# A fused attention, soft-MoE and squared-ReLU kernel on one Trainium2 core: three squares in four of one FFN part go to ScalarE, the last part's weight steps end two steps sooner, one product's parts are made a group sooner

## The chip, the core and the metric

The kernel runs on one core of one Trainium2 chip. The metric is device microseconds of an execution, the median of several runs; lower is better. The times and the profile of the kernel before are from the chip.

## The reference, cut to what matters

```python
x = attention(q, k, v)                 # 4 batches, 8 heads, 768 rows, head size 64
x = soft_moe(x, phi, w1, w2)           # 3072 tokens, width 512, 8 experts of 4 slots
h = x @ w_in                           # 3072x512 @ 512x2048
r = np.maximum(h, 0.0)
g = r * r
out = g @ w_out                        # 3072x2048 @ 2048x512
```

Everything is fp32. The change lies wholly in the last three lines, the FFN (feed-forward network).

## The kernel before, in words

**The FFN.** The 2048 hidden columns are worked in five parts, `WIDTHS = [256, 384, 384, 512, 512]`, numbered q = 0 to 4. The tokens lie in `ND = 6` blocks of 512. Because the MoE output is a product of small factors, `h` for 128 hidden columns and one block is one matmul (`gemm1`, line 1055, into a PSUM tile `h`). The second product is three matmuls of 512 columns per 128 hidden columns: both g and the weights are split into a high and a low fp32r part, and hi·hi, lo·hi (lines 1075, 1076) and hi·lo (line 1084) are summed into a PSUM tile `acc`. For parts 1 to 3, VectorE then adds `acc` into the running output `oacc` (line 1089).

**The gate.** `gate` (lines 1041 to 1049) turns a tile `h` into the two parts of g. ScalarE makes r = relu(h) (line 1043). The full g is made in one of two ways: by ScalarE, as the square of r, in the second half of the same `rg` tile (line 1045), or by VectorE, as max(h, 0)·r, which reads `h` in PSUM again (line 1047). ScalarE then writes the rounded high part (line 1048), and the low part is g minus the high part (line 1049), on GpSimd, or on VectorE for the last block of part 3. The argument `own` of the call on line 1056 chooses the way.

**The loop.** Lines 1325 to 1346 walk parts 0 to 3, six blocks each, four steps (m = 0 to 3) per block; k = 4d + m counts a part's steps from 0 to 23. A step issues one `gemm1` and its gate for the *next* block, then the second product of one 128-row slice of the output. The low products of slice 0 are held until slice 1. Between these, `background` is advanced by a few yields: it loads the next part's weights, converts their 64-bit words to fp32 on ScalarE and VectorE (lines 932 to 937), makes the small factor of `gemm1` (`make_u`), and then splits weights. For part 4 this is `conv_last` (lines 984 to 1009): it makes seven weight operands, with sums and differences (lines 995 and 1004, VectorE), high parts (line 1002, ScalarE) and low parts (line 1008, in turn on VectorE and GpSimd). `total` yields are spread over `room` steps (line 1329).

**The last part.** Part 4 is done by a seven-product scheme (P1, P5, P6, P3, P7, P2, P4) on pairs of token blocks: `pair` (line 1184), three times, each with 14 groups of six matmuls (lines 1207 to 1211), two groups a product; VectorE adds every group into `oacc` (line 1191). The right-hand operands are made from squares `y11, y12, y22, y21` and differences `t1` to `t4` (line 1161, VectorE) of them. `y_steps` (line 1121) is a hand-written table: every action has a slot number, slot 0 is just after group 0 of the pair. `products` makes the two `hy` matmuls of a square (line 1136), `relu` reads them on ScalarE (line 1141), `square` writes the fp32 square (line 1144), `high` its rounded part (line 1148 or 1150, ScalarE), `low` the rest (line 1156, on GpSimd in two halves or on VectorE at once). The first pair's slots from -13 on fall into the last steps of part 3.

Every engine works through its own queue in program order; semaphores hold an instruction until its inputs are there and its output tile is free. `h` and `hy` tiles share the PSUM tags `h`, `k` and `u`: a new one waits until all readers of the old one in its place are done. The `rg` tiles and the `r` tiles of `products` share two SBUF places of the tag `e`.

Of the kernel before, what the change touches and what calls it, by code (L numbers as in the profile page):

```python
# [7 lines left out]
F32 = mybir.dt.float32  # L8
# [12 lines left out]
P = 128  # L21
# [9 lines left out]
TB = 256  # L31
WIDTHS = [256, 384, 384, 512, 512]
QL = len(WIDTHS) - 1
# [7 lines left out]
def attention_moe_ffn(ctx: ExitStack, tc, qk, vx, nn, phi, w1, w2, w_in, w_out, consts, relw, out):  # L41
    nc = tc.nc
    V, G = nc.vector, nc.gpsimd
# [153 lines left out]
    def slot(tag, shape, dt, name):  # L197
        return (pre if tag[0] == "p" else stream).tile(shape, dt, tag=tag, name=name)
# [468 lines left out]
    ph = pl.rearrange("p (t g h s) -> p t h g s", g=2, h=NPR, s=NS)  # L667
# [188 lines left out]
    ex = ctx.enter_context(tc.tile_pool(name="ex", bufs=1, side="right"))  # L856
# [176 lines left out]
    ND = NBLK // 2  # L1033

    def g_of(q, d):
        i = (q * ND + d) % 2
        if i not in gbuf:
            gbuf[i] = slot(("s2", "p2")[i], [P, 2, 4, 2 * TB], F32R, f"g{i}")
        return gbuf[i]

    def gate(q, g2, js, cs, ph, rg, own=False, low=None):
        r, g = rg[:, 0], rg[:, 1]
        nc.scalar.activation(r, ph, AF.Relu)  # L1043
        if own:
            nc.scalar.activation(g, r, AF.Square)
        else:
            V.scalar_tensor_tensor(g, ph, 0.0, r, op0=ALU.max, op1=ALU.mult)  # L1047
        nc.scalar.activation(g2[:, 0, js, cs], r, AF.Square)  # L1048
        (low or (G if q else V)).tensor_tensor(g2[:, 1, js, cs], g, g2[:, 0, js, cs].bitcast(F32), op=ALU.subtract)  # L1049

    def gemm1(q, d, j):
        if j >= WIDTHS[q] // P:
            return
        ph = fps.tile([P, 2 * TB], F32, tag="k" if (q, d) == (QL - 1, ND - 1) else next(hk), name=f"h{q}_{d}_{j}", bufs=2)
        nc.tensor.matmul(ph, lhsT=wq[q]["U"][:, j * P : j * P + P], rhs=cst[:, d * 2 * TB : d * 2 * TB + 2 * TB], start=True, stop=True)  # L1055
        gate(q, g_of(q, d), j, slice(0, 2 * TB), ph, ex.tile([P, 2, 2 * TB], F32, tag="e", name=f"rg{q}_{d}_{j}", bufs=2), q in (1, 2) and j > 0, V if (q, d) == (QL - 1, ND - 1) else None)

    def gemm1_first(n):
        ph = fps.tile([P, 2, TB], F32, tag=next(hk), name=f"h0_0_0_{n}", bufs=2)
# [31 lines left out]
    def gemm2(q, d, m):  # L1091
        if m == 0 and q:
            held[0] = gemm2_hi(q, d, 0)
            return
        pa = gemm2_hi(q, d, m)
        if m == 1 and q:
            gemm2_lo(held[0], q, d, 0)
        gemm2_lo(pa, q, d, m)
# [9 lines left out]
    def region(name, k):  # L1108
        if "t" not in yt:
            yt["t"] = slot("p4", [P, 4, 2, 2 * TB], F32, "yt")  # L1110
        yt[name] = slotZ[:, 0 : 4 * TB].rearrange("p (a c) -> p a c", a=2) if k == 4 else yt["t"][:, k]
        return yt[name]

    def y_parts(name):
        n = PLACE[name]
        if n - n % 2 not in yt:
            yt[n - n % 2] = slot(("p0", "p1", "s2", "p2")[n // 2], [P, 2, 2, 2, 2 * TB], F32R, f"yop{n}")
        t = yt[n - n % 2]
        return t[:, n % 2, 0], t[:, n % 2, 1]

    def y_steps(p):

        a, b = 2 * p, 2 * p + 1
        r, at = {}, {}

        def step(slot_, f, *args):
            at.setdefault(slot_, []).append(lambda: f(*args))

        def products(y, half, chunk):
            r[y] = ex.tile([P, 2, 2 * TB], F32, tag="e", name=f"r{y}_{chunk}", bufs=2)  # L1130
            r[y, "h"] = []
            for jj in range(2):
                j = 2 * half + jj
                tag = next(hhu)
                ph = fps.tile([P, 2 * TB], F32, tag=tag, name=f"h{y}_{chunk}_{jj}", bufs=1 if tag == "u" else 2)
                nc.tensor.matmul(ph, lhsT=wq[QL]["U"][:, j * P : j * P + P], rhs=cst[:, chunk * 2 * TB : chunk * 2 * TB + 2 * TB], start=True, stop=True)
                r[y, "h"].append(ph)

        def relu(y):
            for jj in range(2):  # L1140
                nc.scalar.activation(r[y][:, jj], r[y, "h"][jj], AF.Relu)

        def square(y, k):
            nc.scalar.activation(region(y, k), r[y], AF.Square)

        def high(name, y):
            if y in r:
                nc.scalar.activation(y_parts(name)[0], r[y], AF.Square)  # L1148
            else:
                nc.scalar.copy(y_parts(name)[0], yt[y])  # L1150

        def low(name, y, eng):
            hi, lo = y_parts(name)
            for c in ((0, 1), (1, 2)) if eng is G else ((0, 2),):
                c = slice(*c)
                eng.tensor_tensor(lo[:, c], yt[y][:, c], hi[:, c].bitcast(F32), op=ALU.subtract)  # L1156
            yop[name] = hi, lo

        def diff(y, k, x0, x1):
            x0, x1 = yt[x0], yt[x1]  # L1160
            V.tensor_tensor(region(y, k), x0, x1, op=ALU.subtract)

        for y, half, chunk, slot_ in (("y11", 0, a, -13), ("y12", 0, b, -10), ("y22", 1, b, -7), ("y21", 1, a, -3)):
            step(slot_, products, y, half, chunk)
            step(slot_ + 1, relu, y)
        for y, k, slot_ in (("y11", 0, -10), ("y12", 1, -8), ("y22", 3, -5), ("y21", 1, 0)):
            step(slot_, square, y, k)
        for y, k, x0, x1, slot_ in (("t1", 2, "y12", "y11", -6), ("t2", 0, "y22", "t1", -3), ("t3", 4, "y22", "y12", -2), ("t4", 2, "y21", "t2", 3)):
            step(slot_, diff, y, k, x0, x1)
        for name, y, s0, s1, eng in (("P1", "y11", -9, -7, G), ("P5", "t1", -3, -1, G), ("P6", "t2", 0, 2, V), ("P3", "y22", -2, 1, G),  # L1170
                                     ("P7", "t3", 2, 5, G), ("P2", "y21", 1, 3, G), ("P4", "t4", 6, 8, V)):
            step(s0, high, name, y)
            step(s1, low, name, y, eng)
        return at

    plans = [y_steps(p) for p in range(ND // 2)]

    def make(p, slot_):
        for n in (p, p + 1):
            if n < ND // 2:  # L1180
                for f in plans[n].get(slot_ - (14 if n > p else 0), ()):
                    f()
# [127 lines left out]
    def background(q):  # L1310
        if q > 1:
            load_part(q)
        yield from conv_in(q)
        for _ in range(3):
            yield
        yield from make_u(q)
        if q == QL:
            yield from conv_last()
            return
        for c in conv_out(q):  # L1320
            yield from c
# [3 lines left out]
    for i in range(QL * ND):  # L1325
        q, d = i // ND, i % ND
        if d == 0:
            bg = background(q + 1)
            total, room = 5 * (WIDTHS[q + 1] // P) + (10 if q + 1 == QL else 7), 4 * (ND - 1) - (2 if q + 1 == QL else 1)
        for m in range(4):  # L1330
            k = 4 * d + m
            for _ in range((k + 1) * total // room - k * total // room):
                next(bg, None)
            if k == 4 * (ND - 1) - 2:
                for _ in bg:
                    pass
            if ahead[i]:
                gemm1(*ahead[i], m)
            if q == QL - 1:
                for slot_ in (2 * k - 48, 2 * k - 47):  # L1340
                    if slot_ >= -13:
                        make(0, slot_)
            if i:
                gemm2(q, d, m)
            else:
                next(first_products, None)
# [165 lines left out]
```

## Time and profile before

| | |
|---|---|
| median of 3 runs | 512.85 us (512.21 to 512.89) |
| profiled execution, its own time | 513.21 us |
| span in the trace of that execution | 511.4 us |
| PE (TensorE matmul) busy | 500.3 us, 98% |
| DVE (VectorE) busy | 391.9 us, 77% |
| ACT (ScalarE) busy | 335.3 us, 66% |
| POOL (GpSimd) busy | 158.1 us, 31% |
| TensorE clock granted, mean of the span | 0.999 |

Parts 0 to 3 of the FFN end near 444 us of the span, and the three pairs of part 4 fill the rest. A busy engine is not an engine at its best rate: matmul records overlap, so the rate of TensorE is read from the distance between the starts of matmuls that follow each other, and a stall from a distance that is longer.

### The profile page before, as it was taken

The page shows a single profiled execution, that of the slowest core. Times are in us where ns is not written, and L with a number is a line of the kernel's source. Part 1 is how long each engine was busy: PE and PEld are TensorE (multiplying, and loading weights), DVE is VectorE, ACT ScalarE, POOL GpSimd, SP SyncE. Part 2 cuts the span into 40 slices and gives each one's busy share as a digit, 9 for nine tenths or more (in the row PEclk, how much of TensorE's full clock was granted, in tenths as well). Part 3 has the DMA queues.
Part 4 walks back from the last instruction along what each step waited for, and adds up shares of the span by engine and source line. Part 5 has one row for each costly group of instructions (what it writes and reads, how often), then busy time and mean ns, then how long its engine had stood idle before and what let it go on. Part 6 is the DMA issues. An engine that isn't in the chain of part 4 may idle for free.

```text
span 511.4 us, 9819 instructions
## 1 busy us (share of the span) xinstructions
PE 500.3 (98%) x3517; PEld 382.0 (75%) x3517; DVE 391.9 (77%) x925; ACT 335.3 (66%) x840; POOL 158.1 (31%) x126
## 2 busy tenths in 40 slices
PE   9999999999999999999999999999999998999997
PEld 6777777687777744487887888788887876878785
DVE  7788888787887745688864765788696998579894
ACT  6987877878878402387985856576654566656650
POOL 7000000000000110000454554446644452866691
PEclk9999999999999999999999999999999999999999
DMA  8888999999994799913304040402200000013124
GB/s 278 261 283 295 365 309 326 313 330 314 318 336 139 274 357 420 406 64 126 123 1 164 1 164 2 164 2 67 97 1 1 2 0 1 1 41 124 62 104 164
DMA packets 25975, 86.93 MB, mean 170 GB/s; under 512 B 2882, under 2 KB 5442, under 8 KB 23746
## 3 DMA queue, kind: packets, MB, share of 16 engines
q1 hardware_dynamic: 25776, 86.13, 47.0%
q8 instruction: 29, 0.48, 0.4%
q14 instruction: 24, 0.20, 0.1%
q10 hardware_dynamic: 146, 0.13, 0.1%
HBM read 79.95 MB, written 6.29 MB: 169 GB/s over the span
## 4 chain that ended last, share of the span: by engine, by line
PE 53%; DVE 8%; ACT 1%; issue 0%; DVEq 0%; ACTq 0%
PE acc L1075 10%; PE acc L1076 10%; PE acc L1084 10%; PE pSO L923 3%; PE h L1055 3%; DVE rg L1047 1%; PE b2P L1211 1%; PE b2P L1208 1%; PE b2P L1209 1%; PE b1P L1211 1%; PE b0P L1211 1%; DVE oacc_p L1089 1%; PE b1P L1208 1%; PE b0P L1208 1%; PE b1P L1209 1%; PE b0P L1209 1%
## 5 line engine op out<-in xcount | busy, mean ns | idle before, releaser
L1075 PE MATMUL acc<-g,w 128*128 128x512 f32 x280 | 109.1, 390 | 0.0
L1076 PE MATMUL acc<-g,w 128*128 128x512 f32 x280 | 109.0, 389 | 0.0
L1049 POOL TENSOR_TENSOR g<-rg,g 128x512 fp32r<-128x512 f32 x56 | 75.4, 1352 | 81.8 <-DVE rg L1047 26.5
L263 ACT ACTIVATE sm<-sm,nm 128x256 f32<-128x256 f32 (+1 forms) x192 | 92.7, 487 | 1.3 <-DVE nm L248 1.3
L1084 PE MATMUL acc<-g,w 128*128 128x512 f32 x280 | 75.5, 389 | 0.0
L1043 ACT ACTIVATE rg<-h 128x512 f32<-128x512 f32 (+1 forms) x73 | 43.1, 591 | 44.0 <-PE h L1055 33.9
L248 DVE CUSTOM_DVE_ANT_0 sm<-s,mask 128x256 f32<-128x256 f32 (+1 forms) x192 | 66.8, 397 | 1.9 <-ACT sm L263 1.2
L1076 PEld LDWEIGHTS acc<-g,w 128*128 128x128 f32 x280 | 52.6, 188 | 11.0
L1084 PEld LDWEIGHTS acc<-g,w 128*128 128x128 f32 x280 | 52.6, 188 | 11.0
L1075 PEld LDWEIGHTS acc<-g,w 128*128 128x128 f32 x280 | 52.6, 188 | 10.7
L235 PE MATMUL s<-raw 64*128 64x256 f32 (+1 forms) x384 | 52.9, 397 | 0.0
L1089 DVE TENSOR_TENSOR oacc_p<-acc,oacc_p 128x512 f32<-128x512 f32 x48 | 32.4, 686 | 22.7 <-PE acc L1084 22.7
L673 POOL TENSOR_TENSOR lh<-lh 128x256 f32<-128x256 f32 x1 | 0.7, 731 | 158.4 <-PE pt L274 158.4
L1156 POOL TENSOR_TENSOR yop<-yt,yop 128x512 fp32r<-128x512 f32 x24 | 40.2, 1701 | 25.2 <-ACT yop L1148 9.0
L274 PE MATMUL pt<-con,sm 128*128 128x128 f32 x352 | 45.5, 277 | 1.6 <-ACT pT L280 1.6
L1048 ACT ACTIVATE g<-rg 128x512 fp32r<-128x512 f32 (+1 forms) x73 | 45.4, 621 | 1.6
L291 PE MATMUL o<-pT,v 128*64 128x128 f32 x704 | 44.2, 276 | 0.0
L274 PEld LDWEIGHTS pt<-con,sm 128*128 128x128 f32 x352 | 38.6, 141 | 7.3 <-ACT pT L280 2.8
L291 PEld LDWEIGHTS o<-pT,v 128*64 128x64 f32 x704 | 37.9, 137 | 6.9 <-ACT sm L263 2.1
L235 PEld LDWEIGHTS s<-raw 64*128 64x128 f32 x384 | 32.1, 194 | 14.6 <-DMA v<-in_vx 6.8
L1047 DVE SCALAR_TENSOR_TENSOR rg<-h,rg 128x512 f32<-128x512 f32 (+1 forms) x49 | 32.9, 674 | 9.6 <-ACT rg L1043 9.5
L263 ACT ACTIVATION_READ_ACCUMULATOR sm<-sm,nm 128x1 f32 x192 | 37.0, 193 | 0.0
(289 smaller groups left out, 880.0 us busy)
## 6 DMA issues: line engine op xcount, KB each, us to landing
w<-in_w SPq DMA_DIRECT2D x40, 512.0 KB, 6.6
raw<-in_qk SPq DMA_DIRECT2D x32, 384.0 KB, 5.3
w<-in_w SPq DMA_DIRECT2D x5, 2048.0 KB, 10.0
v<-in_vx SPq DMA_DIRECT2D x32, 256.0 KB, 4.3
raw<-in_qk SPq DMA_DIRECT2D x16, 320.0 KB, 5.1
win<-in_w_in SPq DMA_DIRECT2D x2, 2048.0 KB, 7.9
wout<-in_w_out SPq DMA_DIRECT2D x2, 2048.0 KB, 8.0
out_x<-oacc_p SPq DMA_DIRECT2D x15, 256.0 KB, 2.0
```

The lines of the kernel that those rows point to most:

```text
L235: nc.tensor.matmul(sc[hh][:, tt, 0:n, :], lhsT=r[r0 : r0 + D, tt, :], rhs=rhs, start=True, stop=True)
L248: V.tensor_tensor_reduce(out=sm[:, j, 0:n, :], in0=sc[hh][:, tt, 0:n, :], in1=m[:, 2:3, :] if n == 1 else m[:, 0:2, :], scale=-QK_SCALE, s ...
L263: nc.scalar.activation(sm[:, j, 0:n, :], sm[:, j, 0:n, :], AF.Exp, bias=nm[:, j : j + 1], scale=-1.0, accum_out=chunk_sums(i // NPR)[:, tt ...
L274: nc.tensor.transpose(pp[tt][:, hh, c, :], sm[:, 2 * tt + hh, c, :], ident)
L291: nc.tensor.matmul(o[hh * D : hh * D + D, tt, :], lhsT=v[:, c * 3 if tt == 0 else 1 + c, hh * D : hh * D + D], rhs=pT[:, 2 * tt + hh, c, : ...
L1043: nc.scalar.activation(r, ph, AF.Relu)
L1048: nc.scalar.activation(g2[:, 0, js, cs], r, AF.Square)
L1049: (low or (G if q else V)).tensor_tensor(g2[:, 1, js, cs], g, g2[:, 0, js, cs].bitcast(F32), op=ALU.subtract)
L1075: nc.tensor.matmul(pa, lhsT=whi[:, j, ms], rhs=ghi[:, j, :], start=j == 0, stop=False)
L1076: nc.tensor.matmul(pa, lhsT=wlo[:, j, ms], rhs=ghi[:, j, :], start=False, stop=False)
L1084: nc.tensor.matmul(pa, lhsT=whi[:, j, ms], rhs=glo[:, j, :], start=False, stop=j == J - 1)
L1156: eng.tensor_tensor(lo[:, c], yt[y][:, c], hi[:, c].bitcast(F32), op=ALU.subtract)
```

## The change

Three edits, all to tables or conditions that set who does what and when:

1. The gates of part 3 (`QL` is 4) with j > 0 take the way of line 1045 in place of line 1047, as parts 1 and 2 already do: three gates of four, 18 in all.
2. While part 3 is worked, `room` is 16 in place of 18: the 30 yields that prepare part 4 end two steps sooner.
3. P6's high part moves from slot 0 to slot -1, its low part from slot 2 to slot 1.

```diff
@@ gemm1
-        gate(..., q in (1, 2) and j > 0, V if (q, d) == (QL - 1, ND - 1) else None)
+        gate(..., 0 < q < QL and j > 0, V if (q, d) == (QL - 1, ND - 1) else None)
@@ y_steps
-        for name, y, s0, s1, eng in (("P1", "y11", -9, -7, G), ("P5", "t1", -3, -1, G), ("P6", "t2", 0, 2, V), ("P3", "y22", -2, 1, G),
+        for name, y, s0, s1, eng in (("P1", "y11", -9, -7, G), ("P5", "t1", -3, -1, G), ("P6", "t2", -1, 1, V), ("P3", "y22", -2, 1, G),
@@ loop
-            total, room = 5 * (WIDTHS[q + 1] // P) + (10 if q + 1 == QL else 7), 4 * (ND - 1) - (2 if q + 1 == QL else 1)
+            total, room = 5 * (WIDTHS[q + 1] // P) + (10 if q + 1 == QL else 7), 4 * (ND - 1) - (4 if q + 1 == QL else 1)
```

The queue of VectorE where part 3 meets part 4. The names leave out the part: `rg_4_3` is the tile of part 3, block 4, chunk 3, and `acc_3_2` the sum of part 3, block 3, slice 2; `xs` and `xp` hold the weight operands of part 4. Before:

```order
L1047 SCALAR_TENSOR_TENSOR rg_4_2_11849<-h_4_2_11847,rg_4_2_11849 128x512
L1089 TENSOR_TENSOR oacc_p_10153<-acc_3_2_11854,oacc_p_10153 128x512
L1008 TENSOR_TENSOR xs_11810<-winf_11480,xs_11810 128x512
L1047 SCALAR_TENSOR_TENSOR rg_4_3_11872<-h_4_3_11870,rg_4_3_11872 128x512
L1089 TENSOR_TENSOR oacc_p_10153<-acc_3_3_11877,oacc_p_10153 128x512
L1008 TENSOR_TENSOR xp_11811<-winf_11480,xp_11811 128x512
L1047 SCALAR_TENSOR_TENSOR rg_5_0_11897<-h_5_0_11895,rg_5_0_11897 128x512
L1049 TENSOR_TENSOR g_10196<-rg_5_0_11897,g_10196 128x512
L1008 TENSOR_TENSOR xp_11811<-winf_11480,xp_11811 128x512
L1047 SCALAR_TENSOR_TENSOR rg_5_1_11916<-h_5_1_11914,rg_5_1_11916 128x512
L1049 TENSOR_TENSOR g_10196<-rg_5_1_11916,g_10196 128x512
```

The same place after the change:

```order
L1008 TENSOR_TENSOR xs_11773<-winf_11480,xs_11773 128x512
L1089 TENSOR_TENSOR oacc_p_10153<-acc_3_0_11809,oacc_p_10153 128x512
L1089 TENSOR_TENSOR oacc_p_10153<-acc_3_1_11830,oacc_p_10153 128x512
L1008 TENSOR_TENSOR xp_11774<-winf_11480,xp_11774 128x512
L1089 TENSOR_TENSOR oacc_p_10153<-acc_3_2_11860,oacc_p_10153 128x512
L1008 TENSOR_TENSOR xp_11774<-winf_11480,xp_11774 128x512
L1089 TENSOR_TENSOR oacc_p_10153<-acc_3_3_11884,oacc_p_10153 128x512
L1047 SCALAR_TENSOR_TENSOR rg_5_0_11900<-h_5_0_11898,rg_5_0_11900 128x512
L1049 TENSOR_TENSOR g_10196<-rg_5_0_11900,g_10196 128x512
L1049 TENSOR_TENSOR g_10196<-rg_5_1_11916,g_10196 128x512
```

The products `rg_4_2`, `rg_4_3` and `rg_5_1` have left the queue, and the two low parts `xp` stand ahead of the gates of block 5, where they stood between them.

GpSimd's queue in the same place, before (`g` is the low part of a gate, line 1049):

```order
L1049 TENSOR_TENSOR g_10163<-rg_4_0_11796,g_10163 128x512
L1049 TENSOR_TENSOR g_10163<-rg_4_1_11817,g_10163 128x512
L1008 TENSOR_TENSOR xs_11810<-winf_11480,xs_11810 128x512
L1049 TENSOR_TENSOR g_10163<-rg_4_2_11849,g_10163 128x512
L1049 TENSOR_TENSOR g_10163<-rg_4_3_11872,g_10163 128x512
L1008 TENSOR_TENSOR xs_11810<-winf_11480,xs_11810 128x512
L1008 TENSOR_TENSOR xp_11811<-winf_11480,xp_11811 128x512
```

and after:

```order
L1049 TENSOR_TENSOR g_10163<-rg_4_0_11804,g_10163 128x512
L1008 TENSOR_TENSOR xs_11773<-winf_11480,xs_11773 128x512
L1049 TENSOR_TENSOR g_10163<-rg_4_1_11825,g_10163 128x512
L1008 TENSOR_TENSOR xs_11773<-winf_11480,xs_11773 128x512
L1049 TENSOR_TENSOR g_10163<-rg_4_2_11855,g_10163 128x512
L1008 TENSOR_TENSOR xp_11774<-winf_11480,xp_11774 128x512
L1049 TENSOR_TENSOR g_10163<-rg_4_3_11879,g_10163 128x512
```

All three weight parts now stand ahead of the low part of gate 4_3; one did before.

VectorE's queue in the second pair, where L1156 is P6's low part, and L1191 adds the groups 1, 2 and 3 (`12261`, `12277` or `12278`, `12289`); the other two pairs read alike:

```order
 L1191 TENSOR_TENSOR oacc_p_10153<-b1P_12261,oacc_p_10153 128x512
-L1191 TENSOR_TENSOR oacc_p_10153<-b1P_12277,oacc_p_10153 128x512
 L1156 TENSOR_TENSOR yop_12064<-yt,yop_12064 128x1024
+L1191 TENSOR_TENSOR oacc_p_10153<-b1P_12278,oacc_p_10153 128x512
 L1191 TENSOR_TENSOR oacc_p_10153<-b1P_12289,oacc_p_10153 128x512
 L1161 TENSOR_TENSOR yt<-yt 128x1024
```

P6's low part stood behind the add of group 2 and now stands ahead of it.

## Rows read from the trace of the kernel before

**Rows 1.** Busy time by stretch: PE, PEld, DVE, ACT, POOL; PE clock, DMA share, GB/s.

```profile
388.00:410.00 22.00, 22.00 (x101) 17.26 (x101) 18.01 (x26) 11.89 (x21) 7.79 (x6) 1.00 0.01 1
410.00:433.00 23.00, 20.75 (x90) 16.29 (x88) 22.34 (x28) 13.73 (x24) 10.58 (x7) 1.00 0.00 0
```

**Rows 2.** Timeline of PE, first two waits: start, us, instruction, [idle before <-releaser].

```profile
419.44 0.39 PE L1136 MATMUL hy<-cu 128*128 128x512 f32 x1
420.75 0.50 PE L1136 MATMUL hy<-cu 128*128 128x512 f32 x1 [0.91 <-DVE rg L1047]
421.08 0.39 PE L1075 MATMUL acc<-g,w 128*128 128x512 f32 x1
...
427.69 0.39 PE L1055 MATMUL h<-cu 128*128 128x512 f32 x1
...
431.28 0.39 PE L1136 MATMUL hy<-cu 128*128 128x512 f32 x1
433.05 0.50 PE L1136 MATMUL hy<-cu 128*128 128x512 f32 x1 [1.39 <-ACT ry L1141]
```

**Rows 3.** Timeline of PE, third and fourth wait.

```profile
450.41 0.39 PE L1211 MATMUL b0P<-yop,xs 128*128 128x512 f32 x1
...
451.32 0.39 PE L1209 MATMUL b0P<-yop,xs 128*128 128x512 f32 x1
452.47 0.73 PE L1211 MATMUL b0P<-yop,xs 128*128 128x512 f32 x2 [0.77 <-DVE yop L1156]
...
473.23 0.39 PE L1209 MATMUL b1P<-yop,xs 128*128 128x512 f32 x1
474.26 0.72 PE L1211 MATMUL b1P<-yop,xs 128*128 128x512 f32 x2 [0.64 <-DVE yop L1156]
```

**Rows 4.** Timeline of ACT, 415 to 433 us.

```profile
415.73 0.59 ACT L1043 ACTIVATE rg<-h 128x512 f32<-128x512 f32 x1
...
425.17 0.60 ACT L1043 ACTIVATE rg<-h 128x512 f32<-128x512 f32 x1 [1.71 <-PE h L1055]
...
430.19 0.60 ACT L1043 ACTIVATE rg<-h 128x512 f32<-128x512 f32 x1 [1.57 <-DVE g L1049]
430.82 0.63 ACT L1048 ACTIVATE g<-rg 128x512 fp32r<-128x512 f32 x1
431.36 1.04 ACT L1144 ACTIVATE yt<-ry 128x1024 f32<-128x1024 f32 x1
432.40 1.08 ACT L1141 ACTIVATE ry<-hy 128x512 f32<-128x512 f32 x2
```

**Rows 5.** Timeline of DVE: behind the first two waits, and at P6's low part.

```profile
420.01 0.68 DVE L1047 SCALAR_TENSOR_TENSOR rg<-h,rg 128x512 f32<-128x512 f32 x1
...
429.41 0.69 DVE L1049 TENSOR_TENSOR g<-rg,g 128x512 fp32r<-128x512 f32 x1
...
447.67 0.69 DVE L1191 TENSOR_TENSOR oacc<-b0P,oacc 128x512 f32<-128x512 f32 x1 [0.67 <-PE b0P L1211]
...
450.09 2.33 DVE L1156 TENSOR_TENSOR yop<-yt,yop 128x1024 fp32r<-128x1024 f32 x1
...
469.17 1.27 DVE L1191 TENSOR_TENSOR oacc_p<-b1P,oacc_p 128x512 f32<-128x512 f32 x2
```

**Rows 6.** One line's instructions: xcount: ns min/median/max, first and last start.

```profile
L1045 ACT ACTIVATE rg<-rg x24: 632/633/637, 255.9 to 357.9; 128x512 f32<-128x512 f32 x24
L1156 DVE TENSOR_TENSOR yop<-yt,yop x6: 1216/1270/2330, 450.1 to 501.7; 128x1024 fp32r<-128x1024 f32 x6
```

**Rows 7.** Timeline of POOL.

```profile
410.41 1.58 POOL L1049 TENSOR_TENSOR g<-rg,g 128x512 fp32r<-128x512 f32 x1 [1.32 <-ACT g L1048]
...
414.57 1.75 POOL L1008 TENSOR_TENSOR xs<-winf,xs 128x512 fp32r<-128x512 f32 x1
...
447.54 2.54 POOL L1156 TENSOR_TENSOR yop<-yt,yop 128x512 fp32r<-128x512 f32 x2 [2.02 <-issue]
```

**Rows 8.** Timeline of SP, the last load of weights.

```profile
354.28 0.33 SPq L948 DMA_DIRECT2D wout<-in_w_out  x1
```

More of the change, by code (lines that the diff above doesn't have):

```diff
@@ L1055, in gemm1 @@
         nc.tensor.matmul(ph, lhsT=wq[q]["U"][:, j * P : j * P + P], rhs=cst[:, d * 2 * TB : d * 2 * TB + 2 * TB], start=True, stop=True)
-        gate(q, g_of(q, d), j, slice(0, 2 * TB), ph, ex.tile([P, 2, 2 * TB], F32, tag="e", name=f"rg{q}_{d}_{j}", bufs=2), q in (1, 2) and j > 0, V if (q, d) == (QL - 1, ND - 1) else None)
+        gate(q, g_of(q, d), j, slice(0, 2 * TB), ph, ex.tile([P, 2, 2 * TB], F32, tag="e", name=f"rg{q}_{d}_{j}", bufs=2), 0 < q < QL and j > 0, V if (q, d) == (QL - 1, ND - 1) else None)
     def gemm1_first(n):
```

## The prediction

> **What bounds the kernel now.** I read three views in this order. First the stretches: around the place where part 3 of the FFN meets part 4, TensorE is busy throughout from 388 to 410 us, but only 20.75 of 23 us from 410 to 433 us, and there VectorE is busy 22.34 of the 23 us, while ScalarE has 13.73 us of work [rows 1]. The clock granted is 1.00 in both, the 2.4 GHz level, so TensorE loses there by waiting, not by its clock. Second, TensorE's timeline, for the waits themselves. From part 3 on there are four that matter. Their size is the distance between the starts of two matmuls that follow each other, less what it is without a wait: from 450.41 to 451.32 us four steps take 0.91 us, 0.227 us each [rows 3].
>
> - Wait A: 420.75 - 419.44 - 0.23 = 1.08 us; the matmul after it comes 0.33 us later, 0.10 us over the normal step, so 1.18 us together. A tile `hy` waits for VectorE's L1047 [rows 2].
> - Wait B: 433.05 - 431.28 - 0.23 = 1.54 us, 1.64 us with the same 0.10 us. A tile `hy` waits for a relu of ScalarE, L1141 [rows 2].
> - Waits C and D: 452.47 - 451.32 - 0.23 = 0.92 us in the first pair, 474.26 - 473.23 - 0.23 = 0.80 us in the second, 1.02 and 0.90 us with the 0.10 us. Group 4 waits for P6's low part, L1156 on VectorE [rows 3].
>
> Together 4.74 us. Third, the timelines of the other engines, for what stands behind each wait. TensorE's matmuls themselves are not touched by the change, so these 4.7 us are about all that it can bring.
>
> **Edit 1, the square by ScalarE.** It removes 18 times L1047 from VectorE, 0.68 us each [rows 5], 12.2 us, and adds 18 times L1045 to ScalarE, 0.633 us each (24 of them, 632 to 637 ns) [rows 6], 11.4 us. Neither sum is on TensorE's path by itself. From 388 to 410 us ScalarE works 11.89 us [rows 1]; a step of 13 matmuls takes 13 x 0.227 = 2.95 us, so the stretch has 7.5 steps, 5.6 of them with a square, and 5.6 x 0.633 = 3.5 us more make 15.4 of 22 us. There is room. A gate's full g is also made later, since ScalarE does it between the relu and the high part where VectorE did it beside the high part; the high part comes about 0.55 us later (the distance from 430.82 to 431.36 is what one such activation holds the engine [rows 4]). It is read four and more microseconds after its `h` (thirteen matmuls of the same step, then the next block's first ones), so this is hidden by TensorE's own work; without that cover it would cost 0.55 us a block.
>
> *Wait A.* The tile that `hy` takes over was read by the gate of block 4, chunk 3: by ScalarE at 415.73 us [rows 4], but by VectorE only at 420.01 us [rows 5], behind the weight parts L1008 that fill its queue. After the edit ScalarE alone reads it. Its relu would end by 416.3 us, and `hy` is due at 419.44 + 0.23 = 419.67 us: 3.3 us of slack. Wait A goes whole: 1.18 us.
>
> *Wait B.* The tile is free when the first of the two L1141 at 432.40 us ends, about 433.00 us [rows 4]. They stand behind the gate of block 5, chunk 3, whose relu waited until 430.19 us for VectorE's L1049 at 429.41 us [rows 4, 5], although its `h` was there at 427.69 + 0.39 = 428.08 us [rows 2]. After the change VectorE has lost both products and low parts from here, so that relu can start when `h` is done, if ScalarE is free: the relu of chunk 2 at 425.17 us [rows 4], then square and high part, 0.60 + 0.63 + 0.55, then the two relus of `hy`, 1.08, end at 428.0 us. So it starts at 428.12 us, 2.07 us sooner. One square more stands behind it, 0.55 us. The first L1141 ends at 433.00 - 2.07 + 0.55 = 431.48 us, and TensorE comes to that matmul at 431.28 + 0.23 = 431.51 us. It is a tie: I leave 0.2 us of the 1.64 (a tenth of wait and the restart) and book 1.44 us. Between 0 and the whole wait nothing excludes either end; the chain of rows puts it here.
>
> **Edit 2, the weight steps.** It adds and removes no instruction; it moves the 30 yields from 18 steps to 16, so the last ones come two steps, 5.9 us, sooner. It takes the two low parts `xp` from between the gates of block 5 on VectorE, which wait B needs and where L1049 and L1047 had to queue. The loads are not reached: both are issued by the first yield, in the first step as before, and SP sent the last one at 354.28 us [rows 8], thirty and more microseconds before a conversion of it. What it fills are the steps before 410 us, where VectorE has 18.01 of 22 us [rows 1] and now gives up 5.6 x 0.68 = 3.8 us to edit 1. On GpSimd it puts all three weight parts ahead of the low part of gate 4_3; that is the first rival. By itself I cost it at nothing.
>
> **Edit 3, P6's parts.** ScalarE makes the high part a slot sooner, while it would only wait for the square `y21`'s place, so it costs nothing. The low part leaves its place behind the add of group 2 and follows the add of group 1. In the first pair that add ends at 447.67 + 0.69 = 448.36 us [rows 5]. The low part took 2.33 us there and 1.22 us at best [rows 5, 6]; even with 2.33 us it ends at 450.7 us, and it is due at 451.32 + 0.23 = 451.55 us [rows 3]. In the second pair: 469.17 + 1.27 + 2.33 = 472.8 us against 473.46 us. Both waits go: 1.02 + 0.90 = 1.92 us. The add of group 2 now stands behind it, up to 1.2 us later; its PSUM tile is wanted again four groups later (P3 adds onto P5), 24 x 0.227 = 5.4 us.
>
> **The sum.** 1.18 + 1.44 + 1.92 = 4.54 us. The profiled execution took 513.21 us, 1.8 us of it outside the span, and lies 0.36 us above the median of 512.85 us. Against itself the sum gives 508.7 us, against the median 508.3 us. I predict **508.5 us**.
>
> **Rivals.**
>
> *GpSimd becomes the late one.* From the low part of gate 4_0 at 410.41 us on it now has seven instructions up to that of gate 4_3, each 1.27 us when alone (two in 2.54 us) and up to 1.75 us [rows 7]: the last ends between 419.3 and 422.7 us. The relu of gate 5_1 needs that `rg` place. Wait A gone, the relu of 5_2 is due at 425.17 - 1.18 = 423.99 us, and the chain from 5_1's relu to its low part takes 0.60 + 0.63 + 0.63 + 0.69 = 2.55 us: so GpSimd must be done by 421.4 us, and being 1.2 us late passes on into wait B. Then B keeps some 1.0 us more: 509.5 us. For it: VectorE's traffic there; against it: the middle of the bounds is 421.0 us.
>
> *P6's low part meets GpSimd sooner.* L1156 took 2.33 us beside GpSimd's work and 1.22 us without [rows 5, 6, 7]. Where one of the two waits for the other, GpSimd's own parts for P3, P2 or P7 slip by up to 1.1 us, and a group waits for these instead. In two of three pairs this costs 2.2 us: 510.7 us.
>
> *Both in full*, all three pairs and B: 4.54 - 1.0 - 3.3 leaves 0.2 us, 512.8 us, which is no change. The edits would then only have moved the waits.
>
> *ScalarE becomes the bound*, the case on the other side. If a square cost c, the stretch from 388 to 410 us would need 11.89 + 5.6 c; it is full at c = 1.8 us, and from there ScalarE sets the pace of part 3. At three times VectorE's 0.68 us, c = 2.05 us, it needs 23.4 of 22 us, 6%, over the six blocks' 24 x 2.95 = 71 us: 4.5 us lost. The three squares of block 5 would also lengthen the chain behind B, two of them by 1.4 us each, 2.8 us, where B's own gain is then gone. 512.85 + 4.5 + 2.8 - 1.18 - 1.92 = 517 us. Against it stand 24 squares of just this form at 0.633 us [rows 6]. The Trainium skill (ScalarE: Activation LUTs, Rules for kernel authors) says that relu, max and multiplications belong on VectorE, which it gives as up to about three times faster per element in bf16. By that rule this edit would be wrong; the trace does not agree for fp32 tiles of 512, where the two engines take 0.63 and 0.68 us.
>
> **How the numbers follow.** The forecast has 0.60, GpSimd late 0.21, the meeting at P6 0.10, both in full 0.05, ScalarE 0.04. A measurement of this kernel can tell about 0.2%, 1.03 us. The first three are faster by more: 0.91. The fourth is within: 0.05. Slower: 0.04. The range runs from 507.7 us (all 4.74 us off the median, and the 0.4 us by which single runs differ) to 510.8 us, which takes in the first rival and most of the second.
>
> **What would show it.** After the change no matmul of line 1136 waits for L1047, since `hy`'s places are read by ScalarE alone; one short wait for L1141 stays, under 0.3 us. From 410 to 433 us VectorE is no longer full (about 18 us), ScalarE has some 3 us more, and L1045 appears in part 3 with 0.63 us. The two L1211 no longer wait for L1156 on VectorE. Wrong would be: a wait of TensorE for GpSimd's L1049 or L1156 above 0.5 us, a wait at `h` (line 1055) for ScalarE in part 3, or wait B still above 1 us.

## The result, and the profile after

The changed kernel takes 508.21 us (median of 4 runs, 507.21 to 508.94) against 512.87 us for the kernel before (4 runs, 512.21 to 513.45): ratio 0.9908, 95% interval 0.9895 to 0.992. That is 4.66 us faster; 508.5 us was predicted, from a sum of 4.54 us. Its profiled execution took 508.47 us, with a span of 506.6 us.

The first view to read again is the stretches (PE, PEld, DVE, ACT and POOL busy, then PE's clock, the DMA share and GB/s), as in [rows 1]:

```profile
388.00:410.00 22.00, 22.00 (x99) 18.18 (x98) 19.31 (x25) 15.48 (x29) 8.41 (x6) 1.00 0.01 1
410.00:433.00 23.00, 23.00 (x102) 18.83 (x101) 14.38 (x20) 18.64 (x33) 11.64 (x8) 1.00 0.00 1
```

From 410 to 433 us TensorE is busy all 23.00 us, where it had 20.75. VectorE's load there fell from 22.34 to 14.38 us, and ScalarE's rose by 4.9 us; the prediction had said about 18 us and some 3 us. From 388 to 410 us ScalarE has 15.48 of 22 us; the prediction had worked out 15.4.

The second is TensorE's timeline at the places of waits A and B, as in [rows 2] (start, us, instruction):

```profile
419.73 0.62 PE L1136 MATMUL hy<-cu 128*128 128x512 f32 x2
...
426.98 0.62 PE L1136 MATMUL hy<-cu 128*128 128x512 f32 x2
430.15 0.79 PE L1136 MATMUL hy<-cu 128*128 128x512 f32 x2
```

Two matmuls of `hy` that follow each other without a wait fill 0.62 us, so wait A is gone whole, and of B's 1.64 us the 0.79 - 0.62 = 0.17 us are left. C and D, at group 4 of the first two pairs, are gone too; here the first pair, as in [rows 3]:

```profile
448.71 0.39 PE L1209 MATMUL b0P<-yop,xs 128*128 128x512 f32 x1
448.94 0.62 PE L1211 MATMUL b0P<-yop,xs 128*128 128x512 f32 x2
```

The view of TensorE's waits from 300 us on is empty. The third view is the chain behind B, on ScalarE:

```profile
421.59 0.60 ACT L1043 ACTIVATE rg<-h 128x512 f32<-128x512 f32 x1 [1.23 <-POOL g L1049]
...
424.24 0.60 ACT L1043 ACTIVATE rg<-h 128x512 f32<-128x512 f32 x1 [0.86 <-PE h L1055]
424.87 0.63 ACT L1045 ACTIVATE rg<-rg 128x512 f32<-128x512 f32 x1
425.40 0.62 ACT L1048 ACTIVATE g<-rg 128x512 fp32r<-128x512 f32 x1
425.92 1.06 ACT L1141 ACTIVATE ry<-hy 128x512 f32<-128x512 f32 x2
427.18 0.60 ACT L1043 ACTIVATE rg<-h 128x512 f32<-128x512 f32 x1 [0.19 <-PE h L1055]
```

The last relu, gate 5_3's, now waits for its own `h` and no more for VectorE. The first one, gate 5_1's, waits for GpSimd: that is the prediction's first rival, and here it just fails to cost anything. GpSimd's queue, as in [rows 7]:

```profile
411.00 1.58 POOL L1049 TENSOR_TENSOR g<-rg,g 128x512 fp32r<-128x512 f32 x1 [4.58 <-DVE rg L1047]
412.54 1.75 POOL L1008 TENSOR_TENSOR xs<-winf,xs 128x512 fp32r<-128x512 f32 x1
414.25 1.84 POOL L1049 TENSOR_TENSOR g<-rg,g 128x512 fp32r<-128x512 f32 x1
416.05 1.75 POOL L1008 TENSOR_TENSOR xs<-winf,xs 128x512 fp32r<-128x512 f32 x1
417.75 1.30 POOL L1049 TENSOR_TENSOR g<-rg,g 128x512 fp32r<-128x512 f32 x1
419.00 1.31 POOL L1008 TENSOR_TENSOR xp<-winf,xp 128x512 fp32r<-128x512 f32 x1
420.26 1.30 POOL L1049 TENSOR_TENSOR g<-rg,g 128x512 fp32r<-128x512 f32 x1
```

It works without a pause from 411.00 to 421.56 us; the prediction had said that it must be done by 421.4 us, and everything in this execution stands 0.29 us later (the first `hy` matmul at 419.73 us against 419.44 us), which puts that point at 421.7 us. The chain behind it ends with the low part of gate 5_1 on VectorE:

```profile
423.40 0.69 DVE L1049 TENSOR_TENSOR g<-rg,g 128x512 fp32r<-128x512 f32 x1 [1.30 <-ACT g L1048]
```

It ends at 424.09 us. The `h` of gate 5_2 (started at 423.81 us, 0.39 us long) was done 0.11 us after that, so the relu of gate 5_2 at 424.24 us was still set by its `h`.

### The profile page after: what moved, and what is told of

Same layout as the page of the kernel before. It is cut to its first block, busy times and chain, and to the rows that moved or that the text cites. A ratio compares the mean times of both kernels' runs of the same rounds, so it can differ in the third digit from the quotient of the medians.

```text
span 506.6 us, 9819 instructions
## 1 busy us (share of the span) xinstructions
PE 499.5 (99%) x3517; PEld 382.6 (76%) x3517; DVE 381.1 (75%) x907; ACT 344.4 (68%) x858; POOL 159.7 (32%) x126
## 4 chain that ended last, share of the span: by engine, by line
PE 61%; DVE 0%; issue 0%
PE acc L1075 13%; PE acc L1076 13%; PE acc L1084 13%; PE h L1055 3%; PE pSO L923 3%; PE b2P L1211 1%; PE b2P L1209 1%; PE b2P L1208 1%; PE b1P L1208 1%; PE b0P L1211 1%; PE b1P L1209 1%; PE b0P L1208 1%; PE b1P L1211 1%; PE b0P L1209 1%; PE hy L1136 1%; PE pre L819 1%
## 5 line engine op out<-in xcount | busy, mean ns | idle before, releaser
L1049 POOL TENSOR_TENSOR g<-rg,g 128x512 fp32r<-128x512 f32 x56 | 77.5, 1392 | 76.1 <-DVE rg L1047 21.2
L1156 POOL TENSOR_TENSOR yop<-yt,yop 128x512 fp32r<-128x512 f32 x24 | 41.5, 1757 | 23.8 <-PE hy L1136 11.9
L280 ACT COPY pT<-pt 128x512 f32<-128x512 f32 x46 | 26.5, 578 | 15.3 <-PE pt L274 15.1
```

## The experiments

All runs are of kernels that differ from the one before or the one after in the places shown. Two numbers are read of each: the median, and the waits of TensorE from 400 us on, by the prediction's own measure (distance of starts less the 0.227 us, with the 0.1 us of restart). The waits are the sharper reading: the profiled executions lie up to 1.0 us apart by the first matmul of line 923, ahead of all that is changed (it starts at 200.25 us in the run of edit 2 alone, at 199.26 us in that of edit 3 alone).

**Edit 1 alone.**

```diff
-        gate(..., q in (1, 2) and j > 0, ...)
+        gate(..., 0 < q < QL and j > 0, ...)
```

> Edit 1 alone. By the prediction, wait A goes whole (1.18 us), and wait B goes only in part, since the two low parts xp of part 4's weights still stand between the gates of block 5 on VectorE: B keeps 0.5 to 1.0 us. C and D stay (1.9 us). In all 1.7 to 2.4 us faster than before, near 510.8 us. Rival: the products L1047 alone were what made VectorE late, so that edit 1 frees A and B by itself: 2.6 us faster, 510.2 us, and TensorE's only waits left are C and D.

Measured: 509.98 us against 512.6 us, ratio 0.9956 (0.9942 to 0.997), 2.6 us faster. At `hy` 0.17 us are left, as in the changed kernel; C and D stay, 1.04 and 0.88 us. They are all that the view of TensorE's waits from 300 us on lists (what waited, for what, us, times, longest):

```profile
PE b0P L1211 <- DVE yop L1156: 0.8, 1, 0.8
PE b1P L1211 <- DVE yop L1156: 0.6, 1, 0.6
```

The rival is right in its outcome: taking the products L1047 off VectorE is enough, and A and B go without edit 2. That the products *alone* made VectorE late doesn't follow, as the next run shows.

**Edit 2 alone.**

```diff
-            total, room = ..., 4 * (ND - 1) - (2 if q + 1 == QL else 1)
+            total, room = ..., 4 * (ND - 1) - (4 if q + 1 == QL else 1)
```

> Edit 2 alone. By the prediction it frees a part of wait B at most (up to 1.4 us) and leaves A, C and D: 0 to 1.4 us faster than before, 511.4 to 512.8 us. Rival: with the products L1047 still on VectorE, the weight parts only meet them two steps sooner, and a wait of TensorE of 0.5 us or more turns up between 400 and 418 us, where the trace of before has none, in place of A; then the time does not move by more than 0.5 us.

Measured: 510.93 us, ratio 0.9964 (0.995 to 0.9978), 1.7 us faster. Both expectations fell short. A *and* B are gone, and the wait that the rival spoke of turned up at 415 us, but the time moved by more than the rival's 0.5 us. TensorE's waits from 300 us on, then the timelines of PE and of DVE at the new one:

```profile
PE acc L1075 <- DVE oacc_p L1089: 1.0, 1, 1.0
PE b1P L1211 <- DVE yop L1156: 0.6, 1, 0.6
PE b0P L1211 <- DVE yop L1156: 0.5, 1, 0.5
```

```profile
414.80 0.39 PE L1055 MATMUL h<-cu 128*128 128x512 f32 x1
416.21 0.50 PE L1075 MATMUL acc<-g,w 128*128 128x512 f32 x1 [1.02 <-DVE oacc_p L1089]
```

```profile
413.17 1.79 DVE L1008 TENSOR_TENSOR xs<-winf,xs 128x512 fp32r<-128x512 f32 x1
414.88 0.68 DVE L1047 SCALAR_TENSOR_TENSOR rg<-h,rg 128x512 f32<-128x512 f32 x1
415.48 1.27 DVE L1089 TENSOR_TENSOR oacc_p<-acc,oacc_p 128x512 f32<-128x512 f32 x2
```

The add that frees an `acc` place stands behind a weight part of 1.79 us and a product, and TensorE waits 416.21 - 414.80 - 0.23 = 1.18 us, 1.30 us with the restart. The weight parts come two steps sooner, and VectorE's lateness with them: it is paid once, at another tile, where it was paid twice (A and B, 2.82 us). That is 1.5 us of the 1.7.

**Edit 3 alone.**

```diff
-        ("P6", "t2", 0, 2, V)
+        ("P6", "t2", -1, 1, V)
```

> Edit 3 alone. By the prediction waits C and D go, 1.9 us, and A and B stay as they were: 510.9 us. Rival: the low part of P6 meets GpSimd's parts sooner and a group waits for line 1156 on GpSimd instead, 0.5 us or more in one pair or more: 511.5 us or above.

Measured: 510.3 us, ratio 0.9959 (0.9945 to 0.9973), 2.3 us faster. C and D are gone, A and B stand as before (the two long distances are 1.28 and 1.78 us, 1.30 and 1.77 before), and TensorE waits nowhere for line 1156. The waits are as predicted; the median gained 0.4 us more than the 1.9 us booked, and its interval (1.4 to 2.8 us) holds both.

```profile
PE hy L1136 <- ACT ry L1141: 1.4, 1, 1.4
PE hy L1136 <- DVE rg L1047: 0.9, 1, 0.9
```

**Edits 1 and 3, and edits 2 and 3**, each pair made of the lines shown above.

> Edits 1 and 3, without edit 2. By the prediction B keeps 0.5 to 1.0 us and the rest goes: 0.5 to 1.0 us slower than the changed kernel, 508.7 to 509.2 us. Rival: edit 2 does nothing beside edit 1; the time is that of the changed kernel within 0.3 us (508.2 us), and B is down to 0.2 us as there.

Measured: 507.78 us, ratio 0.9907 (0.9891 to 0.9924). The waits are those of the changed kernel, 0.18 us at the third pair of `hy` and nothing else. The rival is right: beside edit 1, edit 2 is worth nothing that can be seen. The relu of gate 5_1, which waits for GpSimd in the changed kernel, here waits for its own `h`:

```profile
419.03 0.60 ACT L1043 ACTIVATE rg<-h 128x512 f32<-128x512 f32 x1 [0.27 <-PE h L1055]
```

> Edits 2 and 3, without edit 1. Theory: edit 2 takes the weight parts out of the way of A and B, but with all products still on VectorE its queue is late at the add that frees an acc place near 415 us: one wait of 1.3 us there as in the run of edit 2 alone, none at A, B, C and D: 0.9 to 1.3 us slower than edits 1 and 3, 508.9 us. Rival: with edit 3 the delay comes back at A or B: 510 us or more.

Measured: 508.87 us, ratio 0.9934 (0.9912 to 0.9955), with one wait, 1.30 us at the same `acc` matmul as in the run of edit 2 alone, and none at A to D. As the theory said.

**Which of the 18 squares.** Edit 3, with edit 1 for one block of part 3 alone:

```diff
-        gate(..., q in (1, 2) and j > 0, ...)
+        gate(..., 0 < q < QL and j > 0 and (q < QL - 1 or d == ND - 2), ...)
```

> Edit 3, and edit 1 for block 4 of part 3 alone: three squares go to ScalarE, not 18; no edit 2. Theory: only what VectorE gives up in the last microseconds ahead of waits A and B counts. hy's place is free of L1047 there, so A goes (1.2 us); and VectorE is 3 x 0.68 = 2.0 us earlier at the low part of gate 5_2, which is what the relu of gate 5_3 waited for (2.1 us), while that chain has no square more, so B goes too: no wait of TensorE above 0.2 us from 400 us on, the time of the kernel with edits 1 and 3 (507.8 us) or 0.2 us less. Rival: VectorE's lateness is built up over the whole of part 3; then A or B keeps 0.5 us or more.

Measured: 508.08 us, ratio 0.9901 (0.9884 to 0.9917). The timeline of PE:

```profile
419.38 0.62 PE L1136 MATMUL hy<-cu 128*128 128x512 f32 x2
426.63 0.61 PE L1136 MATMUL hy<-cu 128*128 128x512 f32 x2
429.80 1.03 PE L1136 MATMUL hy<-cu 128*128 128x512 f32 x2
```

A is gone, and of B 1.03 - 0.62 = 0.41 us are left, 0.2 us over the expected bound and under the rival's 0.5 us. The relu of gate 5_3 is still late there, by 0.7 us (427.46 us; its `h` was done at 426.79 us). Three squares, the ones of block 4, bring nearly all that 18 bring.

> Edit 3, and edit 1 for block 5 of part 3 alone; no edit 2. Theory: A stays whole, 1.1 to 1.2 us, since the place of hy is still read by VectorE in gate 4_3. B: VectorE gives up the products of gates 5_1 and 5_2, 1.4 us, and the chain behind the relu of 5_3 gets 0.55 us longer, so B goes from 1.5 to 0.6 to 0.8 us. 1.8 us slower than edits 1 and 3 together, 509.6 us. Rival: the products of block 5 alone free B whole, and A alone stays: 509.0 us.

Here the condition reads `d == ND - 1`. Measured: 509.22 us, ratio 0.9922 (0.9906 to 0.9939). The timeline of PE:

```profile
418.93 0.39 PE L1136 MATMUL hy<-cu 128*128 128x512 f32 x1
420.20 0.50 PE L1136 MATMUL hy<-cu 128*128 128x512 f32 x1 [0.88 <-DVE rg L1047]
...
430.53 0.39 PE L1136 MATMUL hy<-cu 128*128 128x512 f32 x1
431.32 0.50 PE L1136 MATMUL hy<-cu 128*128 128x512 f32 x1 [0.41 <-ACT ry L1141]
```

A stays, 1.04 us and restart; B is 0.57 us and restart, 0.67 us. The median lies between the two expectations and doesn't tell them apart; the waits are those of the theory: A stays while VectorE reads the tile of gate 4_3 behind its weight parts, and B shrinks by a part.

**How much room ScalarE has.** The changed kernel with each square of part 3 done twice:

```diff
-            nc.scalar.activation(g, r, AF.Square)
+            for _ in range(2 if q == QL - 1 else 1):
+                nc.scalar.activation(g, r, AF.Square)
```

> The changed kernel, with each square of line 1045 in part 3 done twice by ScalarE, 18 x 0.63 us = 11.4 us more work there; the result is the same. If ScalarE has room in part 3 (15.5 of 22 us worked from 388 to 410 us), TensorE still doesn't wait at h (line 1055) and only the chain into hy grows: the squares of gates 5_2 and 5_3 stand in it, 0.55 us each, so the wait at hy goes from 0.07 us to 1.2 us, with some of it at other places: 1.0 to 2.0 us slower than the changed kernel, about 509.7 us. Rival, ScalarE is nearly the bound: waits of TensorE for ScalarE before 410 us, and 4 us or more.

Measured: 509.45 us, ratio 0.993 (0.9913 to 0.9946), 1.2 us above the changed kernel's median. The waits are at two places (the edit moves lines by one, so L1137 is `hy` and L1049 the high part):

```profile
417.76 0.39 PE L1077 MATMUL acc<-g,w 128*128 128x512 f32 x1
418.77 0.50 PE L1076 MATMUL acc<-g,w 128*128 128x512 f32 x1 [0.62 <-ACT g L1049]
...
430.22 0.39 PE L1137 MATMUL hy<-cu 128*128 128x512 f32 x1
431.35 0.50 PE L1137 MATMUL hy<-cu 128*128 128x512 f32 x1 [0.74 <-ACT ry L1142]
```

TensorE waits nowhere before 410 us, though ScalarE has 17.88 of 22 us there. So ScalarE isn't the bound of part 3. The second squares cost 0.9 us at `hy` and 0.8 us where gate 4_3's high part is read, each with a restart, 1.9 us together. The medians show less of it, 1.2 us; both lie within the 1.0 to 2.0 us expected.

**Edit 3 taken apart**, beside edit 1.

```diff
-        ("P6", "t2", 0, 2, V)
+        ("P6", "t2", 0, 1, V)
```

> Edits 1 and of edit 3 the low part's slot alone (2 to 1); the high part stays at slot 0. Theory: C and D hang on VectorE's queue, not on when the high part is made: both go, and the time is that of edits 1 and 3, 507.8 us within 0.4 us. Rival: the high part, made by ScalarE behind the square y21, is now what the low part waits for; C or D keeps 0.3 us or more.

Measured: 507.74 us, ratio 0.9897 (0.9881 to 0.9914); C and D gone. The low part's place is enough.

> Edit 1, and of edit 3 the high part's slot alone (0 to -1); the low part stays at slot 2. Theory: the low part stands behind the add of group 2 and meets GpSimd as before; C and D stay, 0.4 to 1.0 us each, and the time is that of edit 1 alone, 510.0 us within 0.6 us. Rival: the high part was the late one: 508.2 us.

Here the pair of slots is `-1, 2`. Measured: 508.71 us, ratio 0.9922 (0.9903 to 0.9941). Neither was right: of C and D only the restart of 0.1 us each is left, and a wait of 0.45 us, with its restart 0.56 us, came up in the third pair. VectorE and GpSimd in the first pair, first in the run of edit 1 alone, then in this run:

```profile
446.05 0.69 DVE L1191 TENSOR_TENSOR oacc<-b0P,oacc 128x512 f32<-128x512 f32 x1 [1.12 <-PE b0P L1211]
446.66 2.34 DVE L1156 TENSOR_TENSOR yop<-yt,yop 128x1024 fp32r<-128x1024 f32 x1
```

```profile
446.62 3.52 POOL L1156 TENSOR_TENSOR yop<-slotZ,yop 128x512 fp32r<-128x512 f32 x2
```

```profile
445.94 0.69 DVE L1191 TENSOR_TENSOR oacc<-b0P,oacc 128x512 f32<-128x512 f32 x1 [1.12 <-PE b0P L1211]
446.55 1.41 DVE L1156 TENSOR_TENSOR yop<-yt,yop 128x1024 fp32r<-128x1024 f32 x1
```

```profile
445.58 3.52 POOL L1156 TENSOR_TENSOR yop<-slotZ,yop 128x512 fp32r<-128x512 f32 x2
```

In the run of edit 1 alone a GpSimd instruction starts 0.04 us ahead of P6's low part, which then takes 2.34 us. With the high part made sooner, ScalarE reaches the following parts sooner (its L1148 in this place ends at 442.95 us, where it ended at 443.99 us). GpSimd starts 0.93 us earlier against VectorE's add, 0.36 us ahead of it where it was 0.57 us behind, and the low part meets only the end of an instruction and takes 1.41 us. So C and D had two causes, and taking away either removes them but for the restarts: the place in VectorE's queue, and the moment at which two engines met.

**A square left to VectorE.** Edits 1 and 3, and gate 5_3's square back on VectorE:

```diff
-        gate(..., 0 < q < QL and j > 0, ...)
+        gate(..., 0 < q < QL and j > 0 and (q, d, j) != (QL - 1, ND - 1, 3), ...)
```

> Edits 1 and 3, but the square of gate 5_3 left to VectorE, which has room now. Theory: the chain into hy is 0.55 us shorter, so the last wait of TensorE there (0.07 us and 0.11 us of restart) goes too: 0.2 us faster than edits 1 and 3, 507.6 us, below what a few runs can tell. Rival: VectorE is later with the low part of gate 5_3, and a wait for it turns up at an acc matmul: 508 us or more.

Measured: 507.49 us, ratio 0.9903 (0.9885 to 0.9921). TensorE has no wait at all from 400 us on; the last pair of `hy` fills 0.61 us. It is the lowest median, but not apart from 507.78 us by more than the runs differ.

## Why the prediction was right, point by point

*What bounds it.* Right. TensorE's own work didn't change, and the four waits held nearly all there was to gain: of 4.74 us, 0.17 us are left. Two small waits of before are not in that sum, and they went too: 0.16 us at the second pair of `hy`, where two matmuls without a wait fill 0.62 us,

```profile
427.91 0.78 PE L1136 MATMUL hy<-cu 128*128 128x512 f32 x2
```

and 0.13 us in the third pair, at 500.3 us. From the first `hy` matmul to the last matmul of the kernel TensorE took 88.20 us before and takes 83.11 us, 5.09 us less; the median gained 4.66 us.

*Edit 1, wait A.* Right, 1.18 us booked, and gone whole in every run in which gate 4_3 left VectorE. It goes as well when the weight parts come two steps sooner on VectorE (edit 2 alone), which the prediction did not see.

*Wait B.* The size is right: a tie was worked out, 0.2 us left standing, and 0.17 us stood. The step that failed is the share in it: "It takes the two low parts `xp` from between the gates of block 5 on VectorE, which wait B needs". B goes to 0.2 us without edit 2, with the two low parts still between those gates, and block 4's three squares alone bring it to 0.41 us. The chain was read from its last piece, gate 5_2's low part; what made that late lay further up VectorE's queue. VectorE was full from 410 to 433 us, and three products taken out further up, 2.0 us of work, brought the relu of gate 5_3 from 2.1 us behind its `h` to 0.7 us. That any other 2 us of work ahead of it would do the same is likely, but not shown.

*Edit 2 at nothing.* Right beside edit 1. Alone it is worth 1.7 us, since it moves VectorE's excess to where it is paid once. "Nothing" was the right price only because the other edit came with it.

*VectorE's load.* The forecast of about 18 us from 410 to 433 us fits the products alone (six fewer in that stretch, 4 us). The weight parts of lines 995, 1004 and 1008, too, fell there from 10.5 to 5.0 us: some now stand ahead of 410 us, and those that stay are shorter. The prediction left that out; it did not enter the sum.

*Edit 3.* Right: 1.92 us booked, 2.3 us by the medians of its own run, and C and D gone. The worst duration of before, 2.33 us, was taken for the low part; 1.96 us was the longest after the change. That the high part's slot matters too, by shifting GpSimd, was not foreseen.

*The rivals.* GpSimd late: its work ended 0.1 us ahead of the point at which it would have been paid, so that the rival did not come about was luck. Edit 2 brought that risk and, beside edit 1, no gain. The meeting at P6 for the worse: not seen, no matmul of the changed kernel waits for line 1156. ScalarE as the bound: excluded, since even twice the squares cost 1.2 us. The square of part 3 takes 0.633 us as in parts 1 and 2. The Trainium skill's page ScalarE: Activation LUTs (Rules for kernel authors) would leave multiplications to VectorE, and gives its speed in bf16 as the reason; for these fp32 tiles the trace does not agree, by the same 0.63 against 0.68 us. What decided was which engine had room at 420 us.

*The range* held the time. Like against like, the sum gave 508.7 us for the profiled execution, which took 508.47 us, and 508.3 us for the median, which is 508.21 us; single runs lay from 507.21 to 508.94 us, so the last tenths of the agreement are luck.

## What to carry to other kernels

When the bound engine waits only a few times, list those waits with their sizes: their sum, small ones included, caps the gain of an edit that leaves that engine's work as it is. Each has to be followed up the queue of the engine that is late, past its last piece, to where that queue filled up. An engine that is full just ahead of a hand-over needs a few microseconds less of work there: three moved instructions did nearly what eighteen did. When two edits relieve the same queue, run each alone before giving either a share.

## What the runs showed of the hardware

When P6's low part on VectorE started while GpSimd was inside an instruction of line 1156, it ended 1.08 us after the end of that instruction. In the first pair it took 2.34 us with 1.25 us of the other's left (edit 1 alone), 1.96 us with 0.88 us left (the changed kernel), 1.66 us with 0.58 us left and 1.41 us with 0.33 us left (the two runs of edit 3 taken apart). With GpSimd idle it took 1.22 us. The GpSimd instruction that came next, begun while VectorE was at work, took 2.27 to 2.29 us in these runs, against 1.29 us. In the changed kernel (shortest, median and longest, ns):

```profile
L1156 DVE TENSOR_TENSOR yop<-yt,yop x6: 1216/1588/1960, 445.7 to 496.9; 128x1024 fp32r<-128x1024 f32 x6
L1156 POOL TENSOR_TENSOR yop<-slotZ,yop x6: 1291/1295/2287, 446.5 to 494.0; 128x512 fp32r<-128x512 f32 x6
```

So a shift of GpSimd by 0.93 us took 0.93 us off a VectorE instruction, without any change to that instruction. A low part that must be in time should be planned with the rest of the GpSimd instruction that it may meet, not by its mean.

TensorE pays some 0.1 us more after a wait, short or long: the distance behind it was 0.33 to 0.34 us in every run that had one, against 0.227 us, after waits of 0.07 us as after those of 1.5 us.
